# Shorter transposes for the inner attention tiles, and global probabilities sent behind the local ones, in a fused local/global attention and expert kernel

## The chip, the cores and the metric

The kernel runs on one core of one Trainium2 chip. The metric is the device time of one execution in microseconds (us). A comparison goes by the median of several executions; the kernel before was run three times. The profile comes from one further, recorded execution, whose own time is given beside its span below.

## The reference

There are 8 batches of 8 heads, 512 local tokens, 32 global tokens, head size 64, in float32. Global queries attend to all 544 keys, local queries to the 32 global keys and to the local keys within 32 positions. The rows of all heads are joined and sent through a layer with three first matrices (512 to 768), an elementwise maximum, and an output matrix (768 to 512).

```python
s_g = scale * np.matmul(q_g, k_all.transpose(0, 1, 3, 2))
out_g = np.matmul(sm(s_g), v_all)                     # sm: softmax over the last axis
s_ll = scale * np.matmul(q_l, k_l.transpose(0, 1, 3, 2))
s_ll = np.where(np.abs(pos[:, None] - pos[None, :]) <= 32, s_ll, -1000000000.0)
s_l = np.concatenate([scale * np.matmul(q_l, k_g.transpose(0, 1, 3, 2)), s_ll], axis=-1)
out_l = np.matmul(sm(s_l), np.concatenate([v_g, v_l], axis=2))
...
h = np.maximum(np.maximum(x @ w1, x @ w2), x @ w3)
return (h @ w_out).astype(np.float32)
```

## The kernel before

**Tiles.** Two heads form a pair; there are 32 pairs `p`, and each has 4 tiles `t` of 128 local queries, so 128 tiles `sl` in all, with `t = sl % 4` and `p = sl // 4` from tile 16 on. An outer tile (`t` = 0 or 3) sees 192 keys of each head, an inner tile (`t` = 1 or 2) 224. From pair 8 (tile 32) on, outer tiles are "mixed": the last 64 keys of both heads share one chunk of 128. An inner tile has two chunks for each head, one of 128 keys and one of 96; the other 32 columns of the second chunk meet rows of zeros in the packed values.

**Steps of a tile.** `scores` (L340) multiplies queries and keys on TensorE (L367), takes the masked minimum on VectorE (L370) and the exponential on ScalarE (L372), and scales by the reciprocal sum, mostly on GpSimd (`times`, L124). The result lies in `s`; from tile 16 on a DMA of SyncE's queue copies it into one of two `prob` buffers (L382 and L383 for mixed tiles, L385 for others), in the type that TensorE multiplies in one pass. `trans` (L389) transposes the four chunks of `prob` (three and one of global probabilities in some mixed tiles) into the PSUM bank `T` (L398, L401): the chunk is the loaded operand, the identity the streamed one. ScalarE or VectorE copies `T` to `pt` (L111, L109), VectorE stores the rounding rest beside it (L103). `pv` (L440) multiplies `pt` with the values on TensorE (L464).

**Global queries.** `glob` (L282) computes a pair's global scores in two steps into `sg`, of which there is one buffer; ScalarE copies the first part of each there (L111), VectorE finishes it (L302). `glob_soft` (L306) takes the exponential (L311) and GpSimd scales `sg` (L124). `glob_put` (L328) moves six pieces of `sg` (the table `GPUT`, L45) into the three chunks of a `probg` buffer with 7 DMAs of SyncE's queue (L335, and two at L338). `transg` (L413) transposes chunk 0, 1 or 2 of `probg` (L423) for the tile that comes next: chunk 0 for `t` = 0 and 2, chunk 1 for `t` = 1, chunk 2 for `t` = 3 (L401).

**Order.** The main loop (L585 on) is written tile by tile: in tile `sl` it transposes tile `sl + 1`, computes the scores of tile `sl + 3`, loads and splits operands, multiplies tile `sl` with its values, does a step of the next pair's global scores, and transposes the global probabilities of tile `sl + 1`. Between these steps `fill(n)` puts 4, 4, 3 and 7 matmuls of the expert layer of the batch before (`moe_group`, L503 for the first matrices and L522 for the output), so TensorE has independent work while the other engines make the operands. At the end of each batch of 16 tiles `fill(400)` empties the layer's remaining matmuls. A planner (`least`, L88) picks the engine of each copy, subtraction and scaling by summed costs as the program is written. Waits and the final order on each engine's queue come from the tile framework, which orders instructions by when its own model finds them ready; so two DMAs of SyncE may stand in another order than in the text. SyncE's queue starts its DMAs strictly one after the other, each waiting for its data.

In tile `t` = 2 the loop calls `glob_soft(p + 1)` and sends pieces 0 and 3; in tile `t` = 3 it sends pieces 1, 2, 4 and 5.

Of the kernel before, what the change touches and what calls it, by code (L numbers as in the profile page):

```python
# [10 lines left out]
F32 = mybir.dt.float32  # L11
# [10 lines left out]
NP = H // 2  # L22
# [28 lines left out]
def mixed(p, t):  # L51
    return p >= 2 * NP and t in (0, 3)


def f32(ap):
    return ap.bitcast(F32)


def body(ctx, tc, kin, qin, vin, min_, win, out):
    nc = tc.nc  # L60
    act, dve, pool, pe = nc.scalar, nc.vector, nc.gpsimd, nc.tensor
# [7 lines left out]
    psT = ctx.enter_context(tc.tile_pool(name="psT", bufs=1, space=PSUM))  # L69
# [15 lines left out]
    def spend(e, ns):  # L85
        load[e] += ns
# [18 lines left out]
    def copy(out, a, psum=False):  # L105
        n = width(out)
        c = {"d": n * (1.04 if psum else 0.52) + (160 if psum else 150), "a": n * 0.833 + (150 if psum else 190)}
        if least(c) == "d":
            dve.tensor_copy(out=out, in_=a)  # L109
        else:  # L110
            act.copy(out=out, in_=a)  # L111

    def times(out, a, col, move=False):
        n = width(out)
        c = {"d": n * 0.52 + 125, "a": n * 0.833 + 185}
        if not move:
            c["p"] = n * 1.27 + 150
        e = least(c)
        if e == "d":
            dve.tensor_scalar(out=out, in0=a, scalar1=col, scalar2=None, op0=ALU.mult)  # L120
        elif e == "a":
            act.activation(out=out, in_=a, func=AF.Copy, scale=col)
        else:
            pool.tensor_scalar(out=out, in0=a, scalar1=col, scalar2=1.0, op0=ALU.mult, op1=ALU.mult)  # L124
# [95 lines left out]
    def nat_k(p):  # L220
        if p < NP:
            return kn[p // 2][:, p % 2], qg[0][:, p]
        return kraw[p][:, 0:KW], kraw[p][:, KW:]
# [104 lines left out]
    def glob_put(p, which):  # L328
        if p >= B * NP:
            return  # L330
        s, g = pg[p][0], f32(pgt[p])
        for k in which:
            c0, n, i, h, d0 = GPUT[k]
            if k < 5 or p < 2 * NP:
                nc.sync.dma_start(out=g[64 * h:64 * h + 64, i, d0:d0 + n], in_=s[:, c0:c0 + n])  # L335
            else:
                for j in range(2):
                    nc.sync.dma_start(out=g[64:64 + SG, 2, 64 * j:64 * j + 64], in_=s[SG * j:SG * j + SG, 480:544])  # L338

    def scores(i):  # L340
        if i >= NS:
            return
        sl = ORDER[i]
        p, t = divmod(sl, 4)
        c0, n = WIN[t]

        ps = pm.tile([128, 512], F32, name="pm") if i < 8 else psS.tile([128, 512], F32, name="S")
        s = s4[:, i % 4]
        if i < EARLY:
            sc[i] = s  # L350
        else:
            if len(prob) < 2:
                prob.append(const.tile([128, 2, 256], F32R, name="prob", tag=f"prob{2 + len(prob)}"))
                pool.memset(f32(prob[-1]), 0.0)
            sc[i] = prob[i % 2]
        nm = small.tile([128, 2], F32, name="nm")
        z = small.tile([128, 2], F32, name="z")
        ze = z8[:, i % 4]
        ph = [ps[:, 0:224], ps[:, 224:448]]
        for j in range(2):  # L360
            if i in NATK:

                pe.matmul(ph[j][:, 0:n], lhsT=qraw[i][:, 128 * j:128 * j + 128], rhs=nat_k(p)[0][:, c0:c0 + n],  # L363
                          start=True, stop=True)
                continue
            for a in range(2):
                pe.matmul(ph[j][:, 0:n], lhsT=qs[i][:, a, 128 * j:128 * j + 128],  # L367
                          rhs=kst[p][:, j, c0:c0 + n], start=(a == 0), stop=(a == 1))
        for j in range(2):
            dve.tensor_tensor_reduce(out=s[:, j, 0:n], in0=ph[j][:, 0:n], in1=mask[:, (1, 0, 1, 0)[t], 32 * (t == 0):32 * (t == 0) + n],  # L370
                                     scale=-0.125, scalar=3.0e38, op0=ALU.add, op1=ALU.min, accum_out=nm[:, j:j + 1])
            act.activation(out=s[:, j, 0:n], in_=s[:, j, 0:n], func=AF.Exp, bias=nm[:, j:j + 1], scale=-1.0,  # L372
                           accum_out=ze[:, j, 0:1])
        dve.tensor_reduce(out=z, in_=ze, axis=AX.X, op=ALU.add)
        dve.reciprocal(out=z, in_=z)
        for j in range(2):
            times(s[:, j, 0:n], s[:, j, 0:n], z[:, j:j + 1])
        if i >= EARLY:
            d = f32(sc[i])
            if mixed(p, t):  # L380
                d = d.rearrange("p j x -> p (j x)")
                nc.sync.dma_start(out=d[:, 0:256].rearrange("p (j x) -> p j x", j=2), in_=s[:, :, 0:128])  # L382
                nc.sync.dma_start(out=d[:, 256:384].rearrange("p (j x) -> p j x", j=2), in_=s[:, :, 128:192])  # L383
            else:
                nc.sync.dma_start(out=d[:, :, 0:n], in_=s[:, :, 0:n])  # L385
        spend("d", 2 * (n * 1.04 + 220) + 440)
        spend("a", 2 * (n * 0.833 + 278))

    def trans(sl):  # L389
        if sl >= NS:  # L390
            return
        s = sc.pop(sl)
        ps = psT.tile([128, 512], F32, name="T")
        pr, one = (ps, ident) if sl < EARLY else (ps.bitcast(F32R), identr)
        m = 3 if mixed(*divmod(ORDER[sl], 4)) else 4
        s = s.rearrange("p j x -> p (j x)")
        for x in range(m):
            pe.transpose(pr[:, 128 * x:128 * x + 128], s[:, 128 * x:128 * x + 128], one)  # L398
        p, t = divmod(ORDER[sl], 4)
        if t == 3 and mixed(p, t):  # L400
            pe.transpose(pr[:, 384:512], pgt[p][:, 2], identr)  # L401
        src = ps.rearrange("p (x q) -> p x q", q=128)[:, 0:m]
        if sl < NAT:
            pt = pts[sl] = att.tile([128, 4, 160], F32, name="pt", tag="pt")
            copy(pt[:, 0:m, 0:128], src, True)
        else:
            pt = pts[sl] = att.tile([128, 4, 2, 160], F32R, name="pt", tag="pt")
            copy(pt[:, 0:m, 0, 0:128], src, True)
            sub(pt[:, 0:m, 1, 0:128], src, f32(pt)[:, 0:m, 0, 0:128], True)
        if t == 3 and mixed(p, t):  # L410
            transg(sl, ps[:, 384:512])
# [173 lines left out]
    for sl in range(NS):  # L585
        p, t = divmod(ORDER[sl], 4)
        b = p // NP
        settle(4500)
        if sl == 8:
            mm[0] = moe_local(0, 0, 256)  # L590
        elif sl == 16:
            mm[0] = chain(mm[0], moe_local(0, 256, 256))
        elif sl >= 32 and sl % 16 == 0:
            fill(400)
            mm[0] = moe_local(b - 1)
        n = (7, 6, 5, 9) if sl < 16 else (4, 4, 3, 7)
        trans(sl + 1)
        fill(n[0])
        next_scores(sl + 4 if sl < 12 else max(15, sl + 3))
        if sl >= 16:  # L600
            if t == 2:
                split_k(p + 2)
                load_k(p + 3)
        elif sl in (10, 14):
            load_k(sl // 4 + 2)
        elif sl == 15:
            load_k(6)
        fill(n[1])
        pv(sl)
        if sl < 8:  # L610
            if p < 3:
                if t == 0:
                    glob(p + 1, 0)
                    glob(p + 1, 1)
                else:
                    glob_soft(p + 1)
        elif sl < 16:
            if sl in (12, 13):
                glob(NP, sl - 12)
            elif sl == 14:  # L620
                glob_soft(NP)
        elif t <= 1:
            glob(p + 1, t)
        elif t == 2:
            glob_soft(p + 1)
            if p + 1 >= 2 * NP:
                glob_put(p + 1, (0, 3))
        elif p + 1 >= 2 * NP:
            glob_put(p + 1, (1, 2, 4, 5))
        fill(n[2])  # L630
        transg(sl + 1)
        fill(n[3])
        split_v(sl + 2)
        load_v(sl + 4)
        for _ in range(WS[sl] if sl < len(WS) else 0):
            weight_step()
        if sl < 8:
            if t == 1:
                xs.setdefault(0, []).append(split_x(xr[p][:, 0:2, 0:128]))
        elif sl < 16:  # L640
            if t == 3:
                split_x(xr[p][:, 2:4, 0:128], xs[0][p], 256)
        elif sl % 16 >= 12:
            q = b * NP + sl % 16 - 12
            xs.setdefault(b, []).append(split_x(xr[q][:, :, 0:128]))
# [60 lines left out]
```

## Time and profile before

| | |
|---|---|
| three runs | median 834.85 us (832.93 to 837.02) |
| the profiled execution, its own time | 834.52 us |
| its span, first to last instruction | 832.7 us |
| TensorE matmuls (PE) | 803.1 us busy, 96% of the span |
| TensorE operand loads (PEld) | 680.7 us, 82% |
| VectorE (DVE), ScalarE (ACT), GpSimd (POOL) | 61%, 63%, 62% |
| DMA, all engines | 114 GB/s in the mean |

Read it so: lines with PE are matmuls, with PEld the loading of the operand that stays in the array (they overlap matmuls), SPq is SyncE's queue of DMA issues. In a timeline each line has the start, the length in us, the engine, the line of the kernel, the operation, output and inputs, the shape and a count of merged instructions; a bracket at the end gives idle time before it and what ended it. Matmuls are pipelined, so a line's length is longer than its share of TensorE; the distance from one start to the next is what it costs. The expert layer runs beside attention until about 726 us; after that TensorE has only the layer of the last batch and of the global rows.

### The profile page before, as it was taken

Reading aid. Unit: us, or ns where it says so; the run is one execution under the profiler, and the core shown is the slowest. Engines: PE = TensorE matmul, PEld = TensorE weight load, DVE = VectorE, ACT = ScalarE, POOL = GpSimd, SP = SyncE. Lnnn points to the kernel's source line nnn. Section 1 sums busy time; section 2 is a strip of 40 time slices with the busy share of each in tenths; the row PEclk is TensorE's granted clock in tenths of the full one; section 3 lists DMA queues with packets and bytes.
Section 4 is the critical chain, followed back from the end, with each engine's and each line's share of the span. In section 5 each row is a group of like instructions: output and inputs, shape, how many; then the busy total and the mean of one; then the engine's idle time right before and its main releaser. Section 6 shows DMA issues by size and latency. Waiting matters only on the chain.

```text
span 832.7 us, 16036 instructions
## 1 busy us (share of the span) xinstructions
PE 803.1 (96%) x4620; PEld 680.7 (82%) x4620; DVE 511.4 (61%) x1789; ACT 522.3 (63%) x1495; POOL 513.2 (62%) x725
## 2 busy tenths in 40 slices
PE   7779899899999999999999999999999999999997
PEld 5469789878888888888888888878888888888896
DVE  3778744866776677766775766767666676411121
ACT  5788756777676767776676677776776666411111
POOL 4689836786677667867676676866776664311211
PEclk9999999999999999999999999999999999999999
DMA  7566544443344433343335333443335332100001
GB/s 251 174 221 221 186 148 122 132 133 110 110 115 129 117 104 112 100 149 104 103 106 165 111 96 102 125 127 99 105 93 165 115 86 57 59 13 0 26 26 26
DMA packets 106856, 94.58 MB, mean 114 GB/s; under 512 B 31888, under 2 KB 95248, under 8 KB 106768
## 3 DMA queue, kind: packets, MB, share of 16 engines
q1 hardware_dynamic: 106768, 93.56, 37.2%
q8 instruction: 37, 0.61, 0.3%
q14 instruction: 51, 0.42, 0.2%
HBM read 56.85 MB, written 8.91 MB: 79 GB/s over the span
## 4 chain that ended last, share of the span: by engine, by line
PE 81%; DVE 2%; DMA 1%; issue 1%; ACT 1%; POOL 1%; POOLq 0%; DVEq 0%; ACTq 0%
PE pm L503 48%; PE pm L522 15%; PE O L464 6%; PE S L367 5%; PE T L398 3%; PE S L298 2%; DMA prob<-s 1%; PE S L363 1%; PE O L457 1%; PE S L423 1%; ACT s L372 0%; DMA probg<-sg 0%; DVE s L370 0%; PE T L401 0%; DMA qraw<-q_in 0%
## 5 line engine op out<-in xcount | busy, mean ns | idle before, releaser
L503 PE MATMUL pm<-xs,wh 128*128 128x512 f32 (+1 forms) x1440 | 421.8, 368 | 5.5 <-ACT xs L111 2.4
L503 PEld LDWEIGHTS pm<-xs,wh 128*128 128x128 f32 x1440 | 253.3, 189 | 36.6 <-ACT xs L111 2.9
L503 PE MATMUL pm<-xs,wl 128*128 128x512 f32 (+1 forms) x720 | 264.1, 367 | 1.0 <-POOL wl L177 1.0
L503 PEld LDWEIGHTS pm<-xs,wl 128*128 128x128 f32 x720 | 136.3, 189 | 20.9 <-issue 1.6
L124 POOL TENSOR_SCALAR s<-s,z 128x224 f32<-128x224 f32 (+1 forms) x244 | 104.0, 438 | 67.7 <-ACT lox L111 38.7
L522 PE MATMUL pm<-woh,h 128*128 128x512 f32 x408 | 133.4, 398 | 0.9 <-POOL h L103 0.9
L372 ACT ACTIVATE s<-s,nm 128x224 f32<-128x224 f32 (+1 forms) x256 | 118.0, 462 | 19.2 <-DVE nm L370 18.0
L103 POOL TENSOR_TENSOR h<-m,h 128x512 fp32r<-128x512 f32 (+1 forms) x60 | 68.3, 1138 | 98.4 <-ACT h L111 98.2
L511 DVE TENSOR_TENSOR m<-pm,m 128x512 f32<-128x512 f32 (+1 forms) x120 | 72.9, 608 | 71.1 <-PE pm L503 70.7
L103 DVE TENSOR_TENSOR pt<-T,pt 128x512 fp32r<-128x512 f32 (+2 forms) x126 | 70.2, 557 | 72.1 <-ACT pt L111 71.7
L103 POOL TENSOR_TENSOR qs<-qraw,qs 128x256 fp32r<-128x256 f32 x100 | 73.0, 738 | 57.0 <-ACT qs L111 41.9
L370 DVE CUSTOM_DVE_ANT_0 s<-S,mask 128x224 f32<-128x224 f32 (+1 forms) x240 | 80.5, 369 | 28.3 <-PE S L363 17.0
L522 PEld LDWEIGHTS pm<-woh,h 128*128 128x128 f32 x408 | 74.5, 188 | 14.0 <-POOL h L103 1.7
L111 ACT CAST pt<-T 128x512 fp32r<-128x512 f32 (+2 forms) x117 | 55.6, 476 | 48.1 <-PE T L398 41.9
L522 PE MATMUL pm<-wol,h 128*128 128x512 f32 x204 | 81.8, 401 | 1.2 <-POOL wol L177 1.2
L103 POOL TENSOR_TENSOR kst<-kraw,kst 64x576 fp32r<-64x576 f32 x50 | 71.6, 1431 | 14.0 <-DVE nm L370 7.9
L103 POOL TENSOR_TENSOR vs<-vraw,vs 128x256 fp32r<-128x256 f32 x102 | 75.5, 740 | 6.4 <-ACT vs L111 4.8
L464 PEld LDWEIGHTS O<-pt,vs 128*128 128x128 f32 x408 | 66.0, 188 | 8.6
L464 PE MATMUL O<-pt,vs 128*128 128x320 f32 (+1 forms) x408 | 72.8, 300 | 0.0
L111 ACT CAST qs<-qraw 128x256 fp32r<-128x256 f32 x99 | 40.2, 407 | 48.4 <-PE S L367 45.9
L367 PEld LDWEIGHTS S<-kst,qs 128*128 128x128 f32 x400 | 59.6, 190 | 9.1 <-DVE nmg L302 0.6
L111 ACT CAST h<-m 128x512 fp32r<-128x512 f32 (+1 forms) x60 | 33.4, 556 | 53.3 <-DVE m L511 53.3
(99 smaller groups left out, 1228.2 us busy)
## 6 DMA issues: line engine op xcount, KB each, us to landing
vraw<-v_in SPq DMA_DIRECT2D x64, 256.0 KB, 3.2
qraw<-q_in SPq DMA_DIRECT2D x100, 128.0 KB, 2.2
prob<-s SPq DMA_DIRECT2D x56, 224.0 KB, 2.4
wraw<-w_in SPq DMA_DIRECT2D x24, 512.0 KB, 3.6
out_dram<-o SPq DMA_DIRECT2D x32, 256.0 KB, 2.6
kraw<-k_in SPq DMA_DIRECT2D x25, 320.0 KB, 3.4
prob<-s SPq DMA_DIRECT2D x48, 128.0 KB, 2.2
prob<-s SPq DMA_DIRECT2D x48, 64.0 KB, 2.0
```

The costliest lines, as they stand in the source:

```text
L103: (dve if least(c) == "d" else pool).tensor_tensor(out=out, in0=a, in1=b, op=ALU.subtract)
L111: act.copy(out=out, in_=a)
L124: pool.tensor_scalar(out=out, in0=a, scalar1=col, scalar2=1.0, op0=ALU.mult, op1=ALU.mult)
L298: pe.matmul(ps[:, 0:n], lhsT=qgz.rearrange("p j x -> p (j x)")[:, 128 * j:128 * j + 128], rhs=kst[p][:, j, c0:c0 + n], start=(j == 0), sto ...
L367: pe.matmul(ph[j][:, 0:n], lhsT=qs[i][:, a, 128 * j:128 * j + 128], rhs=kst[p][:, j, c0:c0 + n], start=(a == 0), stop=(a == 1))
L370: dve.tensor_tensor_reduce(out=s[:, j, 0:n], in0=ph[j][:, 0:n], in1=mask[:, (1, 0, 1, 0)[t], 32 * (t == 0):32 * (t == 0) + n], scale=-0.12 ...
L372: act.activation(out=s[:, j, 0:n], in_=s[:, j, 0:n], func=AF.Exp, bias=nm[:, j:j + 1], scale=-1.0, accum_out=ze[:, j, 0:1])
L398: pe.transpose(pr[:, 128 * x:128 * x + 128], s[:, 128 * x:128 * x + 128], one)
L464: pe.matmul(o[:, j, 0:320].rearrange("p (a q) -> p a q", a=2)[:, :, 0:n], lhsT=vs[sl][:, 2 * j + c].rearrange("p a d -> p (a d)"), rhs=pt[ ...
L503: pe.matmul(ps[:, 0:n], lhsT=w[f][:, i, k], rhs=xs[k][:, a, c0:c0 + n], start=(q == 0), stop=(q == 11))
L511: dve.tensor_tensor(out=m[:, 0:n], in0=ps[:, 0:n], in1=m[:, 0:n], op=ALU.max)
L522: pe.matmul(ps, lhsT=hh[f][:, a, 128 * t:128 * t + 128], rhs=w[:, f], start=(q == 0), stop=(q == 17))
```

## The change

From tile 34 on an inner tile's two second chunks (`x` odd, four chunks in all) are transposed with 96 loaded columns in place of 128, and the result fills 96 partitions of `T`. The copies out of `T` still read 128 partitions, so the bank must hold finite numbers there: from tile 32 on the same `T` tile is used again and again rather than a new one being allocated each time, and tile 33 still writes all rows.

The DMA of a tile's probabilities is remembered (`sent`). For pairs from 8 on, pieces 1 and 4 of the global probabilities become one DMA. Pieces 0 and 3 are sent in tile `t` = 2 as before. Pieces 1 with 4, and 2, now are sent in tile `t` = 2 too, but on SyncE's queue behind the DMA of the local probabilities of tile `sl + 3` (which is `t` = 1 of the next pair); piece 5 (two DMAs) is sent in tile `t` = 3, behind those of the tile after that. `tc.issue_after` orders the issue on that queue only; it waits for no data.

```diff
@@ glob_put
             c0, n, i, h, d0 = GPUT[k]
+            if k == 1 and p >= 2 * NP:
+                nc.sync.dma_start(out=g[0:64, 1:3, 32:128], in_=s[:, 0:512].rearrange("p (i x) -> p i x", i=2)[:, :, 128:224])
+                continue
             if k < 5 or p < 2 * NP:
...
+    sent = [None]
...
@@ scores
-                nc.sync.dma_start(out=d[:, 256:384].rearrange("p (j x) -> p j x", j=2), in_=s[:, :, 128:192])
+                sent[0] = nc.sync.dma_start(out=d[:, 256:384].rearrange("p (j x) -> p j x", j=2), in_=s[:, :, 128:192])
             else:
-                nc.sync.dma_start(out=d[:, :, 0:n], in_=s[:, :, 0:n])
+                sent[0] = nc.sync.dma_start(out=d[:, :, 0:n], in_=s[:, :, 0:n])
...
@@ trans
-        ps = psT.tile([128, 512], F32, name="T")
+        if sl <= 32:
+            bank[0] = psT.tile([128, 512], F32, name="T")
+        ps = bank[0]
...
-            pe.transpose(pr[:, 128 * x:128 * x + 128], s[:, 128 * x:128 * x + 128], one)
+            w = 96 if sl >= 34 and m == 4 and x % 2 else 128
+            pe.transpose(pr[0:w, 128 * x:128 * x + 128], s[:, 128 * x:128 * x + w], one)
...
@@ main loop
             if p + 1 >= 2 * NP:
                 glob_put(p + 1, (0, 3))
+                with tc.issue_after(sent[0].ins):
+                    glob_put(p + 1, (1, 2))
         elif p + 1 >= 2 * NP:
-            glob_put(p + 1, (1, 2, 4, 5))
+            with tc.issue_after(sent[0].ins):
+                glob_put(p + 1, (5,))
```

More of the change, by code (lines that the diff above doesn't have):

```diff
@@ L382, in scores @@
                 nc.sync.dma_start(out=d[:, 0:256].rearrange("p (j x) -> p j x", j=2), in_=s[:, :, 0:128])
-                nc.sync.dma_start(out=d[:, 256:384].rearrange("p (j x) -> p j x", j=2), in_=s[:, :, 128:192])
+                sent[0] = nc.sync.dma_start(out=d[:, 256:384].rearrange("p (j x) -> p j x", j=2), in_=s[:, :, 128:192])
             else:
-                nc.sync.dma_start(out=d[:, :, 0:n], in_=s[:, :, 0:n])
+                sent[0] = nc.sync.dma_start(out=d[:, :, 0:n], in_=s[:, :, 0:n])
         spend("d", 2 * (n * 1.04 + 220) + 440)
         spend("a", 2 * (n * 0.833 + 278))
+    bank = [None]
     def trans(sl):
```

## The prediction

> **What bounds the kernel now.** I read the page first: busy shares, granted clock, the chain.
>
> ```profile
> span 832.7 us, 16036 instructions
> PE 803.1 (96%) x4620; PEld 680.7 (82%) x4620; DVE 511.4 (61%) x1789; ACT 522.3 (63%) x1495; POOL 513.2 (62%) x725
> PEclk9999999999999999999999999999999999999999
> PE 81%; DVE 2%; DMA 1%; issue 1%; ACT 1%; POOL 1%; POOLq 0%; DVEq 0%; ACTq 0%
> ```
>
> TensorE holds 96% of the span and 81% of the chain at full clock; the others are near 62%. The change touches the stretch from tile 32 on, so I asked the windows view for 200 to 700 us, ten stretches of 50.
>
> ```profile
> sum 500.00, PE 498.12 PEld 422.36 DVE 347.21 ACT 351.45 POOL 345.69; mean PE 49.81 PEld 42.24 DVE 34.72 ACT 35.15 POOL 34.57
> ```
>
> Of 500 us TensorE stands still for 1.88. So no wait that ends earlier can give much, and a gain must come from these stalls or from TensorE's own instructions. The TensorE timeline shows the stalls: three of 0.3 us or more, all ahead of the transposes of an inner tile with t = 1 at the end of a batch. I lay an undisturbed tile beside them, and the tiles' single transposes.
>
> ```profile
> 411.45 0.22 PE L423 MATMUL S<-identr,probg 128*128 128x128 f32 x1
> 411.51 0.45 PE L503 MATMUL pm<-xs,wl 128*128 128x512 f32 x1
> 411.80 0.63 PE L503 MATMUL pm<-xs,wh 128*128 128x512 f32 x2
> 412.26 0.39 PE L503 MATMUL pm<-xs,wl 128*128 128x512 f32 x1
> ...
> 412.95 0.40 PE L503 MATMUL pm<-xs,wl 128*128 128x512 f32 x1
> 413.19 0.46 PE L398 MATMUL T<-identr,prob 128*128 128x128 f32 x4
> 413.49 0.70 PE L503 MATMUL pm<-xs,wh 128*128 128x512 f32 x2
> 414.02 0.39 PE L503 MATMUL pm<-xs,wl 128*128 128x512 f32 x1
> ...
> 452.79 0.39 PE L522 MATMUL pm<-wol,h 128*128 128x512 f32 x1
> 453.71 0.51 PE L398 MATMUL T<-identr,prob 128*128 128x128 f32 x4 [0.54 <-DMA prob<-s]
> ...
> 545.17 0.39 PE L522 MATMUL pm<-wol,h 128*128 128x512 f32 x1
> 546.69 0.51 PE L398 MATMUL T<-identr,prob 128*128 128x128 f32 x4 [1.14 <-DMA prob<-s]
> ...
> 638.41 0.40 PE L522 MATMUL pm<-wol,h 128*128 128x512 f32 x1
> 639.00 0.51 PE L398 MATMUL T<-identr,prob 128*128 128x128 f32 x4 [0.20 <-DVE xs L109]
> ```
>
> An expert matmul ahead of transposes takes 413.19 - 412.95 = 0.24 us. The three stalls are the excess over that: 0.92 - 0.24 = 0.68, 1.52 - 0.24 = 1.28 and 0.59 - 0.24 = 0.35, together 2.31 us. These are tiles 81, 97 and 113.
>
> **The global transfers.** SyncE's queue and the scaling on GpSimd around tile 81, the issues of tiles 97 and 113, and how long the transfers take from issue to landing (minimum, median, maximum; local ones first):
>
> ```profile
> 445.35 3.78 SPq L335 DMA_DIRECT2D probg<-sg  x5
> 449.17 1.23 SPq L338 DMA_DIRECT2D probg<-sg  x2
> 450.50 0.53 SPq L260 DMA_DIRECT2D qraw<-q_in  x1
> 451.13 0.68 SPq L385 DMA_DIRECT2D prob<-s  x1
> ...
> 446.64 0.88 POOL L124 TENSOR_SCALAR s<-s,z 128x224 f32<-128x224 f32 x2
> ...
> 543.85 0.68 SPq L385 DMA_DIRECT2D prob<-s  x1
> ...
> 636.41 0.68 SPq L385 DMA_DIRECT2D prob<-s  x1
> ...
> DMA to landing us min/median/max: 2.0/2.3/5.3
> ...
> DMA to landing us min/median/max: 1.7/1.9/4.7
> ```
>
> GpSimd has tile 81's probabilities ready at 446.64 + 0.88 = 447.52, but the queue sends them at 451.13, behind seven global transfers and a load: 3.61 us late. The transposes start 453.71 - 451.13 = 2.58 after the issue, tile 113's 639.00 - 636.41 = 2.59 and tile 97's 2.84: the same distance, so tile 113 waits for its transfer too, though the row puts it down to another engine. The change leaves pieces 0 and 3 ahead and puts the rest behind, so tile 81 is sent at 447.52 and lands near 447.52 + 2.45 = 450.0, where TensorE could take it at 452.79 + 0.24 = 453.03: 3 us in hand. I take all three stalls away, -2.31 us (end of the bound: nothing, if another wait takes their place, below). What is late next is TensorE itself, since the expert matmuls are in its queue.
>
> What moves, and what it passes. Of seven issues per pair two stay, one merged DMA and piece 2 go behind the t = 1 transfer, and piece 5's two behind the t = 2 transfer, on SyncE's queue alone; GpSimd's scaling of sg is not moved. The merged DMA saves one issue, 0.6 us of SyncE by the rows above (1.23 for two); no user is left that waits for the queue's pace, so it counts nothing. Pieces 1, 2 and 4 are issued by about 448.2 + 2 x 0.6 = 449.4 and land by 451.3; their first user, the t = 1 tile's global transpose, comes 411.45 - 407.22 = 4.23 us after its transposes by the next rows, so near 457.3: 6 us in hand. Piece 5 is the one that becomes late, with who waits for it:
>
> ```profile
> 406.42 0.65 SPq L385 DMA_DIRECT2D prob<-s  x1
> 407.19 0.54 SPq L272 DMA_DIRECT2D vraw<-v_in  x1
> ...
> 407.22 0.45 PE L398 MATMUL T<-identr,prob 128*128 128x128 f32 x4
> ...
> 411.35 0.47 ACT L111 COPY sg<-S 64x384 f32<-64x384 f32 x1
> 413.69 0.59 ACT L111 CAST pt<-T 128x512 fp32r<-128x512 f32 x1
> ...
> 414.31 0.69 DVE L103 TENSOR_TENSOR pt<-T,pt 128x512 fp32r<-128x512 f32 x1 [1.18 <-ACT pt L111]
> ...
> 415.85 0.74 PE L464 MATMUL O<-pt,vs 128*128 128x320 f32 x4
> ```
>
> The one sg buffer is written again by ScalarE at 411.35, and that copy now has to wait until piece 5 has been read. Piece 5's second issue starts at 406.42 + 0.65 + 0.61 = 407.68, or 408.22 behind the load of vraw, and lands 1.9 later, at 409.6 to 410.1: 1.2 us ahead of the copy. Queued behind the copy on ScalarE is the cast of 413.69; VectorE's subtraction ends at 415.00 and TensorE needs it at 415.85, another 0.85. So zero, with 2 us of cover.
>
> **The 96 columns.** Affected are 47 inner tiles (tile 34, and two in each of the 23 pairs 9 to 31), 2 transposes each, 94. The loaded chunk gets narrower; the streamed identity keeps 128 columns, so only the load can gain. What a transpose costs: one alone 0.06 to the next matmul, and that one then 0.29 in place of 0.46 / 2 = 0.23, so 0.12 us. Four: 0.30, and the pair behind takes 414.02 - 413.49 = 0.53 in place of 0.46, so 0.37. Each further transpose costs (0.37 - 0.12) / 3 = 83 ns, more than the 60 ns that the streaming of a single one takes: the loads pace them. Load times by width, from the groups by shape:
>
> ```profile
> L503 PEld LDWEIGHTS pm<-xs,wh 128*128 128x128 f32 x1440 | 253.3, 189 | 36.6 <-ACT xs L111 2.9 <-POOL xs L103 2.6 <-issue 2.1
> L398 PEld LDWEIGHTS T<-identr,prob 128*128 128x128 f32 x400 | 45.9, 141 | 21.0 <-DVE xs L109 2.5 <-issue 1.8 <-DVE xr L472 1.4
> L457 PEld LDWEIGHTS O<-pt,vraw 128*64 128x64 f32 x208 | 12.7, 139 | 6.2 <-ACT pt L111 2.4 <-issue 1.4 <-ACT wct L162 0.2
> L398 PEld LDWEIGHTS T<-ident,s 128*128 128x128 f32 x64 | 7.3, 142 | 2.7 <-issue 2.5 <-ACT pt L111 0.2
> ```
>
> Loads of ordinary matmuls: 189 for 128 columns, 139 for 64, so 0.78 ns a column on a fixed 89. A transpose's 141 is then 89 + 52, or 0.41 a column. No row has a transpose of 96. Upper end of the gain: the ordinary price, 32 x 0.78 = 25 ns, 94 of them 2.35 us. Lower end: the narrower load falls back to the ordinary load's pace, 89 + 96 x 0.78 = 164, which is 23 ns more, +2.2 us. I take the transpose's own price, since the row is this very instruction: 32 x 0.41 = 13 ns, -1.2 us. The Trainium skill (TensorE: Matmul & The Clock Gate, section LDWEIGHTS) prices a load at its columns over 1.2, by which 32 columns are 26.7 ns and the 94 are 2.5 us, an estimate, so that the sum would be -4.8; the 64-column row agrees with it for ordinary loads (0.78 a column), the transposes' 141 does not.
>
> The kept bank: a new T tile waits for the copies of the last, and the kept one waits for the same two readers. VectorE's subtraction of one tile ends at 415.00, and tiles come 413.19 - 407.22 = 5.97 us apart, so some 4 us hide it: zero. Copies, multiplications with the values and the expert layer keep their sizes.
>
> Sum against the profiled execution: 834.52 - 2.31 - 1.2 = 831.0. The median of the runs is 0.33 above that execution, so I forecast **831.4**, 0.42% less than 834.85. I call anything within 0.5% (4.2 us) no change, about what a measurement can tell here.
>
> **The rivals.**
> Faster (0.25): the load is priced by column as for ordinary matmuls. -2.31 - 2.35 = -4.66, 830.2. For it speaks that loads pace the transposes at 83 ns, a quarter of which is 21; against it the 141.
>
> Stalls change their name (0.11): at a batch's end another wait takes the place. For it: the bracket of 639.00 names the cast of xs. Against it: TensorE's first matmuls there read the first of four pieces of x. Only the 1.2 stays: 833.7.
>
> Narrow loads lose (0.11): the lower end, -2.31 + 2.2 = -0.1, 834.7. The Trainium skill (same page, section on weight-path perf modes) says that fast weight load is on only for 128 weights of a type other than FP32, by which 96 would lose it. The trace speaks against that cause: float32 transposes load in 142, the other type's in 141, and the 128-column load of L503 takes 189.
>
> Slower (0.08): piece 5 is too late for ScalarE. It decides once piece 5 lands after 411.35 + 0.85 = 412.2. With vraw ahead and the longest landing of the row, 408.22 + 4.7 = 412.9, so TensorE would wait 0.7 us in each of 23 pairs, 16.1 us: 834.85 + 16.1 - 3.5 = 847.5. For it: sg has one buffer, and the order on the queue is the framework's. Against it: a landing takes 1.9 in the median.
>
> **How the numbers follow.** The forecast has 0.45. Its 3.5 us lie 0.7 from the bound, and three runs of before spread from 832.93 to 837.02, so a median can be off by about 1: I count 0.1 of the forecast's share as faster. Faster 0.25 + 0.1 = 0.35; same 0.35 + 0.11 + 0.11 = 0.57; slower 0.08. The range reaches from the first rival less that 1 to the third plus 1: 829.2 to 835.7. It leaves out the slower rival and some of the ends.
>
> **What would show it.** Right: in the changed profile the three batch ends show 0.24 us ahead of the transposes, waits of L398 on prob are gone, SyncE sends L385 of t = 1 right when GpSimd ends, TensorE's idle time from 200 to 700 us falls below 0.5, and 96-column loads take near 128 ns. Wrong: loads of 164 or more; a wait of ScalarE's sg copy on a DMA and of L464 on pt; or stalls at 453, 545 and 638 us with another name. More than 5 us either way would mean that a cost which I set to zero is not.

## The result and the profile after

The kernel after took 828.88 us in the median of 6 runs (828.43 to 831.59), the kernel before 834.24 beside it (6 runs, 832.93 to 837.02). The ratio is 0.994, with a 95% interval from 0.9921 to 0.9958: 5.4 us less, or 0.6%, where 3.5 us were forecast. The profiled execution took 828.43 us. Its page begins:

```profile
span 826.6 us, 15915 instructions
...
PE 797.9 (97%) x4620; PEld 677.2 (82%) x4620; DVE 514.0 (62%) x1789; ACT 521.8 (63%) x1495; POOL 513.8 (62%) x725
...
PE 83%; DMA 1%; DVE 1%; ACT 1%; POOL 1%; issue 1%; POOLq 0%; ACTq 0%; DVEq 0%
```

TensorE still holds nearly all of the span with the same 4620 matmuls, and 83% of the chain; VectorE, ScalarE and GpSimd stay near 62%. What changed has to be read stage by stage. The windows view from 200 to 700 us, in stretches of 50, ends with:

```profile
sum 500.00, PE 499.93 PEld 424.20 DVE 350.65 ACT 353.68 POOL 346.79; mean PE 49.99 PEld 42.42 DVE 35.06 ACT 35.37 POOL 34.68
```

TensorE stands still for 0.07 us of 500, where it stood for 1.88 before. The three batch ends in TensorE's timeline:

```profile
449.83 0.39 PE L532 MATMUL pm<-wol,h 128*128 128x512 f32 x1
450.06 0.44 PE L408 MATMUL T<-identr,prob 128*128 128x128 f32 x4
...
541.47 0.39 PE L532 MATMUL pm<-wol,h 128*128 128x512 f32 x1
541.70 0.44 PE L408 MATMUL T<-identr,prob 128*128 128x128 f32 x4
...
633.11 0.39 PE L532 MATMUL pm<-wol,h 128*128 128x512 f32 x1
633.34 0.42 PE L408 MATMUL T<-identr,prob 128*128 128x128 f32 x4
```

(All line numbers behind L340 have moved by 5 to 10: the transposes' L398 is now L408.) Each transpose starts 0.23 us behind the expert matmul; before, it was 0.92, 1.52 and 0.59. SyncE's queue around the first of them, and GpSimd's scaling of that tile:

```profile
442.43 1.16 SPq L338 DMA_DIRECT2D probg<-sg  x2
443.68 0.55 SPq L260 DMA_DIRECT2D qraw<-q_in  x1
444.47 0.63 SPq L390 DMA_DIRECT2D prob<-s  x1
445.19 0.62 SPq L335 DMA_DIRECT2D probg<-sg  x1
445.86 1.23 SPq L338 DMA_DIRECT2D probg<-sg  x1
```

```profile
443.56 0.88 POOL L124 TENSOR_SCALAR s<-s,z 128x224 f32<-128x224 f32 x2
```

GpSimd ends at 443.56 + 0.88 = 444.44 and the transfer is sent at 444.47, 0.03 us later in place of 3.61. The merged piece (L335) and piece 2 stand behind it. The loads by shape, from 200 to 720 us (busy us, mean ns of one):

```profile
L408 PEld LDWEIGHTS T<-identr,prob 128*128 128x128 f32 x225 | 29.4, 141 | 8.5 <-DMA prob<-s 0.6
...
L408 PEld LDWEIGHTS T<-identr,prob 128*96 128x96 f32 x90 | 11.4, 126 | 4.0
```

A 96-column load takes 126 ns, a 128-column one still 141. The first row also shows something new, a wait for `prob`. It belongs to the batch's last tile (`t` = 3), whose probabilities come in two transfers; TensorE around it, and the queue:

```profile
438.59 0.39 PE L532 MATMUL pm<-wol,h 128*128 128x512 f32 x1
438.82 0.58 PE L408 MATMUL T<-identr,prob 128*128 128x128 f32 x3
439.24 0.25 PE L411 MATMUL T<-identr,probg 128*128 128x128 f32 x1
```

```profile
436.27 0.66 SPq L387 DMA_DIRECT2D prob<-s  x1
437.03 0.65 SPq L388 DMA_DIRECT2D prob<-s  x1
```

The first chunks are there in time. The third chunk comes with L388, issued at 437.03 right behind L387; it lands at 439.08, its load starts at 439.12, and TensorE waits in the middle of the tile: 439.24 - 438.82 = 0.42 us for three transposes, which elsewhere take 0.22. Four batch ends have it, and their excess of about 0.2 each sums to 0.8 us.

**Where the time went.** I cut the trace by the first multiplication with the values of tile 32 and of tile 127, which is nearly all that the change touches. Before, then after:

```profile
180.86 0.30 PE L464 MATMUL O<-pt,vs 128*128 128x320 f32 x1
...
725.37 0.30 PE L464 MATMUL O<-pt,vs 128*128 128x320 f32 x1
```

```profile
178.55 0.30 PE L474 MATMUL O<-pt,vs 128*128 128x320 f32 x1
...
719.53 0.30 PE L474 MATMUL O<-pt,vs 128*128 128x320 f32 x1
```

The stretch takes 544.51 before and 540.98 after, 3.53 us less. Another 2.31 lie ahead of tile 32, where the compute engines run the same instructions in both kernels; only SyncE's queue differs there, from 173 us on, by the transfers of pair 8. So in the stretch these two executions give what was forecast, and the 2.31 need an explanation of their own: chance, or something that the change does early on. The runs below settle that too.

### The profile page after: what moved, and what is told of

Read it like the earlier page. It is cut to its first block, busy times and chain, and to the rows that moved or that the text cites. A ratio compares the mean times of both kernels' runs of the same rounds, so it can differ in the third digit from the quotient of the medians.

```text
span 826.6 us, 15915 instructions
## 1 busy us (share of the span) xinstructions
PE 797.9 (97%) x4620; PEld 677.2 (82%) x4620; DVE 514.0 (62%) x1789; ACT 521.8 (63%) x1495; POOL 513.8 (62%) x725
## 4 chain that ended last, share of the span: by engine, by line
PE 83%; DMA 1%; DVE 1%; ACT 1%; POOL 1%; issue 1%; POOLq 0%; ACTq 0%; DVEq 0%
PE pm L513 48%; PE pm L532 16%; PE O L474 6%; PE S L372 5%; PE T L408 3%; PE S L298 1%; DMA prob<-s 1%; PE S L368 1%; PE S L433 1%; PE O L467 0%; ACT s L377 0%; PE T L411 0%; POOL s L124 0%; DVE kst L109 0%; PE S L294 0%
## 5 line engine op out<-in xcount | busy, mean ns | idle before, releaser
L474 PEld LDWEIGHTS O<-pt,vs 128*128 128x128 f32 x408 | 66.0, 188 | 8.5
L474 PE MATMUL O<-pt,vs 128*128 128x320 f32 (+1 forms) x408 | 72.7, 299 | 0.0
```

The costliest lines, as they stand in the source:

```text
L474: pe.matmul(o[:, j, 0:320].rearrange("p (a q) -> p a q", a=2)[:, :, 0:n], lhsT=vs[sl][:, 2 * j + c].rearrange("p a d -> p (a d)"), rhs=pt[ ...
```

## The experiments

**The change again, and its parts.** Four kernels were timed beside the kernel before (29 runs, median 834.75): the change as it is; the sending order alone; the narrow transposes with the kept bank alone; the kept bank alone.

> The whole change once more, beside the kernel before. Theory A (the sum of the prediction holds, -3.5 us, and what was measured beyond it lies ahead of tile 32, where no instruction differs, as spread between executions): from the first multiplication with values of tile 32 to that of tile 127 the trace is 3.3 to 3.8 us shorter than that of before (544.5 us), and the medians differ by 3 to 4.5 us. Rival B (the change is worth 5 to 6 us by itself): the medians differ by 5 us or more again, whatever the time of tile 32.

The order alone has the change's `glob_put` and main loop (the merged transfer is part of it and has no run of its own), with

```diff
-        if sl <= 32:
-            bank[0] = psT.tile([128, 512], F32, name="T")
-        ps = bank[0]
+        ps = psT.tile([128, 512], F32, name="T")
...
-            w = 96 if sl >= 34 and m == 4 and x % 2 else 128
+            w = 128
```

> The global transfers merged and sent behind the local ones; transposes with 128 columns and a new T bank for each tile, as before. Theory A: the three waits at the batch ends are gone, -2.3 us from tile 32 to tile 127, medians -2 to -3. Rival B1 (the extra gain comes from the transfers): -4 us or more. Rival C (the narrow transposes carry the gain, the stalls come back elsewhere): within 0.8 us of before.

The narrow transposes alone undo the sending:

```diff
-            if k == 1 and p >= 2 * NP:
-                nc.sync.dma_start(out=g[0:64, 1:3, 32:128], ...)
-                continue
...
-                with tc.issue_after(sent[0].ins):
-                    glob_put(p + 1, (1, 2))
...
-            with tc.issue_after(sent[0].ins):
-                glob_put(p + 1, (5,))
+            glob_put(p + 1, (1, 2, 4, 5))
```

> 96 columns and the kept bank; transfers in the order of before. Theory A: -1.2 us from tile 32 to 127 (13 ns for each of 94 loads), with the waits at the batch ends still there, longer by what TensorE is earlier. Rival B2 (narrow loads gain as much as ordinary ones, 25 ns or more): -2.4 us or more.

The kept bank alone is that kernel with `w = 128`.

> The T bank kept from tile 32 on, with 128 columns in all transposes and the transfers of before. Theory A: no change, within 0.5 us from tile 32 to 127. Rival B3 (a new bank for each tile costs a wait that the trace puts elsewhere): -1 us or more.

| kernel | median us (runs) | ratio to before, 95% | stretch, tile 32 to 127 | TensorE idle, 200 to 700 us |
|---|---|---|---|---|
| whole change | 829.05 (6) | 0.9932 [0.9908, 0.9955] | 541.42 | 0.07 |
| order alone | 831.74 (12) | 0.9961 [0.9945, 0.9977] | 542.03 | 0.00 |
| narrow, kept bank | 831.69 (12) | 0.9970 [0.9955, 0.9985] | 543.04 | 1.86 |
| kept bank alone | 833.26 (12) | 0.9987 [0.9970, 1.0004] | 544.66 | 2.06 |

The whole change is 5.7 us faster in the median, more than the 3 to 4.5 of theory A, while its stretch is only 544.51 - 541.42 = 3.09 shorter, less than the 3.3 of that theory. Both parts are worth something, and each leaves the other's cost standing: the order alone has no idle time at all, the narrow transposes alone keep batch ends' stalls (1.7 and 0.5 us in this trace). Here is the stall in the narrow kernel (TensorE's waits for 200 to 720 us: engine, line, releaser, us in total, times, longest):

```profile
PE T L405 <- DMA prob<-s: 1.5, 1, 1.5
```

The kept bank's 544.66 is the 544.51 of before again, and its interval reaches 1.0004, so no effect is established, although its median is 1.5 us lower.

**How much two executions of one kernel differ.** The kernel before was recorded three times more and the change twice more, to compare four traces with four.

> The kernel before, recorded a second time, to see how far one execution differs from another. Theory A (the changed stretch is steady, the start is not): tile 32 to tile 127 takes 544.5 us within 0.4 again, while tile 32 comes anywhere from 178.5 to 181 us. Rival B4 (the kernel before has a slower start than the others by itself): tile 0 again near 18.3 us and tile 32 near 180.9, where the five other traces have tile 0 at 15.9 to 16.6.

> The kernel before, a third recorded execution. Open is why the medians differ by 5.4 and 5.7 us where the recorded stretches from tile 32 to 127 differ by 3.1 to 4.3. Theory A: that stretch takes 544.5 to 545.3 us again, and an execution's total varies with when tile 32 comes (178.5 to 181). Rival B5 (some executions of the kernel before have longer waits ahead of the transposes, which the change removes): the stretch takes 546 us or more.

> The whole change, a third recorded execution. Theory A: 540.9 to 541.5 us from tile 32 to 127, tile 32 anywhere from 178.5 to 181. Rival B6 (the change also shortens the stretch ahead of tile 32): tile 32 below 179 us, as in the first recorded execution, and not near 180 as in the second.

> The kernel before, a fourth recorded execution, with the same two expectations as the third: Theory A 544.5 to 545.3 us from tile 32 to 127; rival B5 546 us or more.

> The whole change, a fourth recorded execution, with the same two expectations as the third: Theory A 540.9 to 541.5 us from tile 32 to 127 with tile 32 anywhere from 178.5 to 181; rival B6 tile 32 below 179 us.

| trace | start of tile 32 | stretch | batch-end stalls in it |
|---|---|---|---|
| before, recorded first | 180.86 | 544.51 | 2.36 |
| before, second | 179.41 | 545.24 | 3.06 |
| before, third | 181.06 | 544.96 | 2.86 |
| before, fourth | 178.97 | 546.19 | 4.12 |
| change, recorded first | 178.55 | 540.98 | 0 |
| change again | 180.06 | 541.42 | 0 |
| change, third | 178.62 | 541.28 | 0 |
| change, fourth | 180.82 | 541.28 | 0 |

Four things follow. Most of the start belongs to neither kernel: the kernel before has it at 178.97 and the change at 180.82. It goes with the early part of an execution, though no run shows that part as its cause. TensorE's granted clock from 20 to 100 us was 0.98 in the three traces with the earliest start (178.55, 178.62, 178.97) and 0.89 to 0.96 in the other five; and the first trace of before already began its first multiplication with values, that of tile 0, at 18.26 us, the seven others between 15.97 and 16.73. So of the first pair's 2.31 us, 1.93 were there at tile 0. (In the second trace of before tile 0 comes at 16.12, so the late start is not that kernel's own.)

A small part of the start is the change's. From the first multiplication with the values in `vs` (tile 26) to tile 32 the four traces of before, the narrow kernel and the kept bank take 32.11 to 32.18 us, the four of the change and the order alone 31.88 to 31.91. One more batch end lies there, ahead of the transposes of tile 33, before and then after:

```profile
177.74 0.40 PE L522 MATMUL pm<-wol,h 128*128 128x512 f32 x1
178.14 0.51 PE L398 MATMUL T<-identr,prob 128*128 128x128 f32 x4
```

```profile
175.65 0.39 PE L532 MATMUL pm<-wol,h 128*128 128x512 f32 x1
175.88 0.46 PE L408 MATMUL T<-identr,prob 128*128 128x128 f32 x4
```

The transfer of this tile is issued 2.50 us ahead of its transposes before (at 175.64) and 3.23 us ahead after (at 172.65). So 0.24 us of the gain lie ahead of tile 32. The stretch does belong to the kernels: 545.22 in the mean against 541.24, which is 3.98 us less, with the nearest two 3.09 apart. And the stalls of before are longer in every other trace than in the one on which the prediction was made: 3.10 in the mean of four. They are all that its traces differ by there: less its stalls each stretch takes 542.07 to 542.18 us. The fourth trace has a fourth stall, and 1.5 us at each of two others. These are TensorE's waits there, 200 to 720 us:

```profile
PE T L398 <- DMA prob<-s: 3.5, 4, 1.4
```

The whole spans differ by 4.7 us in the mean of four (832.55 and 827.88), which lies inside what the timed runs give, 3.5 to 6.6 us by the interval of the ratio; 0.6 of it lies in the start (0.24 by the change, the rest by chance), 0.1 behind tile 127. The traces thus give the change 4.3 us; the medians' 5.4 and 5.7 are about 1.2 more, which no trace locates.

**Piece 5 still later.** Its cover was set to 2 us without a trace of it. Six small transfers into a tile of zeros, each about 0.6 us of SyncE's queue, were put ahead of it:

```diff
+            for k in range(6):
+                with tc.issue_after(sent[0].ins):
+                    sent[0] = nc.sync.dma_start(out=zero[16 * k:16 * k + 16], in_=ident[16 * k:16 * k + 16, 127:128])
             with tc.issue_after(sent[0].ins):
                 glob_put(p + 1, (5,))
```

> The whole change, with six tiny transfers of 64 bytes put ahead of piece 5 on SyncE's queue, so that piece 5 is read some 3 to 3.6 us later. It tests the cover that the prediction gave that step: 1.2 us until ScalarE's copy into sg and 0.85 more until TensorE. Theory A: ScalarE's copy waits, TensorE stands 1.0 to 1.5 us in each of 23 pairs, 23 to 35 us more than the change. Rival D (ScalarE's work behind that copy has more room than the prediction saw): less than 5 us more.

It took 839.91 us in one run (before: 834.28), and its stretch 550.41, 9.2 more than the change's mean: 0.40 us in each of 23 pairs. Piece 5 without the delay, SyncE and then ScalarE in the change:

```profile
403.43 0.61 SPq L390 DMA_DIRECT2D prob<-s  x1
404.09 1.25 SPq L341 DMA_DIRECT2D probg<-sg  x2
```

```profile
408.33 0.48 ACT L111 COPY sg<-S 64x384 f32<-64x384 f32 x1
```

Its second issue starts at 404.09 + 0.62 = 404.71, 3.6 us ahead of the copy, and no wait stands before the copy. With the delay, SyncE, ScalarE, VectorE and TensorE:

```profile
390.96 1.22 SPq L643 DMA_DIRECT2D zero<-ident  x2
392.23 1.22 SPq L341 DMA_DIRECT2D probg<-sg  x2
```

```profile
394.89 0.48 ACT L111 COPY sg<-S 64x384 f32<-64x384 f32 x1 [1.76 <-DMA probg<-sg]
```

```profile
395.40 0.55 DVE L302 CUSTOM_DVE_ANT_0 sg<-S,sg 64x384 f32<-64x384 f32 x1 [2.08 <-ACT sg L111]
```

```profile
395.19 0.40 PE L513 MATMUL pm<-xs,wh 128*128 128x512 f32 x1
396.01 0.69 PE L372 MATMUL S<-kst,qs 128*128 128x192 f32 x4 [0.43 <-DVE nmg L302]
```

ScalarE stands 1.76 us for the transfer, VectorE for ScalarE, and TensorE 0.43 for VectorE, which frees the PSUM buffer `S` that the next tile's scores need. TensorE's multiplication with `pt` (L474), where the prediction saw the end of the cover, waits nowhere. The waits of all its loads ahead of those scores:

```profile
PEld S L372 <- DVE nmg L302: 12.0, 17, 1.0
```

So the chain is real and begins at the copy, but it reaches TensorE over another buffer. Of 3.7 us of delay 0.40 arrive, neither the full delay nor nothing: the 23 to 35 us of theory A were missed, and so were the less than 5 of rival D.

**All four chunks narrow.** `w = 96 if sl >= 34 and m == 4 else 128`: twice as many narrow loads. It leaves out the last 32 keys of each first chunk.

> The whole change, with 96 loaded columns in all four transposes of an inner tile in place of two. It leaves out the last 32 keys of each first chunk (their rows hold values of an earlier tile). Theory A (loads pace the transposes, 33 ns less per inner tile for two narrow loads): four narrow loads give up to as much again, 0.7 to 1.6 us less from tile 32 to 127. Rival E (the 60 ns of streaming is now the floor): within 0.3 us of the change.

It took 827.66 us in one run, its stretch 539.80, 1.4 less than the change's mean; the change's four traces spread over 0.44. The transposes and the two expert matmuls behind them, in the change and then here:

```profile
404.23 0.43 PE L408 MATMUL T<-identr,prob 128*128 128x128 f32 x4
404.50 0.69 PE L513 MATMUL pm<-xs,wh 128*128 128x512 f32 x2
405.03 0.40 PE L513 MATMUL pm<-xs,wl 128*128 128x512 f32 x1
```

```profile
410.35 0.41 PE L408 MATMUL T<-identr,prob 128*96 128x128 f32 x4
410.61 0.69 PE L513 MATMUL pm<-xs,wh 128*128 128x512 f32 x2
411.14 0.39 PE L513 MATMUL pm<-xs,wl 128*128 128x512 f32 x1
```

From the first transpose to the last row it was 414.02 - 413.19 = 0.83 us before; it is 0.80 with two narrow chunks and 0.79 with four. Over all inner tiles from 200 to 700 us the medians, start to start, up to the second matmul behind, are:

| loads | transposes and the first matmul behind, ns | up to the second matmul |
|---|---|---|
| four of 128 (before) | 60, 66, 84, 85, 302 | 600 |
| two of 96 (change) | 59, 60, 73, 70, 302 | 566 |
| four of 96 | 60, 62, 60, 64, 303 | 548 |

The first two narrow loads save 34 ns a tile, the next two only 18: with all four narrow every transpose follows in 60 to 64 ns, as long as the stream of one takes, and by these medians little is left to win from narrower loads. They account for 18 ns x 47 tiles = 0.85 of the 1.4 us; the rest is not located.

**The same two steps earlier.** Pairs 5 to 7 also send their later pieces behind the local transfer, the narrow chunks begin at tile 17, and the bank is kept from tile 16 on:

```diff
-        if p < 2 * NP:
+        if p == NP:
...
+        elif p < 2 * NP:
+            glob_put(p, (0, 3))
+            with tc.issue_after(sent[0].ins):
+                glob_put(p, (1, 2, 4, 5))
...
-            w = 96 if sl >= 34 and m == 4 and x % 2 else 128
+            w = 96 if sl >= 17 and ORDER[sl] % 4 in (1, 2) and x % 2 else 128
```

> The whole change, and the same two steps for earlier tiles: narrow transposes from tile 17 on, and for pairs 5 to 7 pieces 1, 2, 4 and 5 issued behind the local transfer. In the trace of the change tile 29's probabilities wait 1.45 us behind two global transfers, and TensorE stands 0.9 us for them. Theory A: that stall goes, and 16 narrow loads give 0.25 us: 0.5 to 1.2 us less than the change. Rival F (ahead of tile 32 other engines set the pace): no difference to the change within 0.4 us.

829.90 us (6 runs), a ratio to before of 0.9943 [0.9925, 0.9961]: no better than the change. Tile 32 starts at 181.00 us, in the span of the other starts, and the stretch behind it takes 540.75. TensorE's waits from 140 to 178 us, in the change and then here:

```profile
PE T L408 <- DMA prob<-s: 2.5, 4, 1.0
PE pm L532 <- POOL h L103: 0.9, 1, 0.9
PE S L372 <- DVE nmg L302: 0.4, 1, 0.4
```

```profile
PE T L412 <- DMA prob<-s: 1.9, 2, 1.1
PE T L412 <- ACT pt L111: 1.7, 1, 1.7
PE pm L536 <- POOL h L103: 1.0, 1, 1.0
```

Two of the four waits on the transfer go, and one of 1.7 us on ScalarE's copy takes their place. From tile 26 to tile 32 this trace takes 30.76 us, 1.1 less than the change's four, but the 1.7 us wait stands ahead of tile 26, and from 143.3 to 146.8 us TensorE's granted clock was 0.51. So a local gain is there, and it does not reach the median of six runs; in this early part other engines are late too.

## Why the prediction was right in its mechanism and short in its sum

**The three stalls: right, and too small.** The transfer goes out right behind GpSimd, the stalls are gone in all four traces of the change, and the order alone removes them. The -2.31 us were those of one trace; the mean of four is -3.10. The fourth batch end, at 178 us, lies ahead of the 200 us from which the prediction looked, and adds 0.24. The row at 639.00, which the prediction read as a wait for the transfer although its bracket names an engine, went with the others. The rival in which a stall only changes its name has no row in its favour at those tiles; at `t` = 3 it has 0.6 us, as follows.

**What is late next: missed.** The prediction said that TensorE itself is next, since the first user had 3 us in hand. It looked at the tiles with `t` = 1 alone, and it put SyncE's pace under the new order at nothing. The batch's last tile now gets its second transfer too late, four times 0.2 us. Two things add up there. With the new order the two transfers of a `t` = 3 tile are issued more slowly; these are the ones of the same tile before:

```profile
439.37 0.59 SPq L382 DMA_DIRECT2D prob<-s  x1
440.05 0.59 SPq L383 DMA_DIRECT2D prob<-s  x1
```

The second follows the first by 0.69 us there, by 437.03 - 436.27 = 0.76 in the change, and its landing moves back by 0.12 against the end of GpSimd's scaling. Why the issues became longer (0.59 to 0.66), no run shows. And with narrow loads TensorE arrives 0.03 to 0.08 us earlier. Means over the four batch ends, in us:

| kernel | landing behind GpSimd's end | transposes start behind it | excess of the `t` = 3 transposes over their median time, summed |
|---|---|---|---|
| before, four traces | 2.70 | 2.60 to 2.62 | 0.13 to 0.22 |
| kept bank alone | 2.70 | 2.59 | 0.26 |
| narrow, kept bank | 2.70 | 2.55 | 0.39 |
| order alone | 2.82 | 2.61 | 0.63 |
| change, four traces | 2.82 to 2.83 | 2.56 to 2.57 | 0.79 to 0.82 |
| all four narrow | 2.82 | 2.53 | 0.94 |

In the order alone TensorE starts no earlier than before, so there the whole excess comes from the later landing.

**The narrow loads: right, and near in size.** 126 ns were measured, 128 foretold. But the prediction took only the load's own difference, 13 ns, and 94 of them; in the chain of starts each is worth 17, for the transposes behind each other are paced by the loads: 34 ns x 47 tiles = 1.6 us in place of 1.2. That is the upper end of what the runs say. The narrow kernel's stretch is 544.66 - 543.04 = 1.6 below the kept bank's, but 0.4 of it are shorter stalls in its trace and 0.1 go into longer waits at `t` = 3, which leaves 1.3 to 1.4; the change against the order alone gives 542.03 - 541.24 + 0.2 = 1.0. So 1.2 lies inside. The ordinary price of 25 ns a load was not reached. It was drawn from two rows of different types, too: the 64-column load has float32 operands (`vraw`), the 128-column one does not. By the Trainium skill (TensorE: Matmul & The Clock Gate, section LDWEIGHTS) 32 columns fewer save 26.7 ns, an estimate; the rows give 141 - 126 = 15, so the trace does not agree for transposes. The rival after the Trainium skill (same page, section on weight-path perf modes), that fewer than 128 weights load more slowly, has fallen with the same 126.

**Two zeros held.** The kept bank is not told apart from nothing. Piece 5 costs nothing as it is sent now. Its cover is there, but it ends at another place than the prediction named: at the scores that wait for `S`, not at L474; and when it is used up, TensorE loses a part of the delay rather than all of it.

**The sum.** -3.1 for the stalls, -1.0 to -1.6 for the loads, +0.6 for the new waits (0.8 less the 0.2 that before has in the mean) make -3.5 to -4.1; the stretch gives 541.24 - 545.22 = -3.98, and 0.24 come ahead of it. The forecast had -3.5. What failed is the size of the first term, and the missing third one offset most of it. That the first two traces gave 3.53 was luck: against the same trace of the change the other three of before give 3.98 to 5.21. The median of 828.88 lies 0.3 under the range; 834.85 times the ratio, 829.8, lies inside it. The likeliest outcome of the forecast, no change, was narrowly missed: 0.6%, with an interval from 0.4 to 0.8% that holds the bound of 0.5. The order alone came out 0.5 us better in its one trace than its terms make (3.19 against 3.10 less 0.45 of new waits). Less their stalls the traces of before agree within 0.11 us, so this is not their spread; it stays open, and with it whether the loads are worth 1.0 or 1.6.

## What to carry to other kernels

Where a queue issues strictly in order, look for transfers that have 6 us in hand standing ahead of one that the bounding engine waits for, and price the fix by the stalls of several recorded executions: a stall's place mostly repeats, its length doesn't. When such a stall goes, follow the next tiles' transfers too: the new order can make one of them land later, and the engine may arrive earlier at it. Narrower loads pay where start-to-start times show that loads pace the engine, and only down to the time of the stream.

## What was not expected of the hardware

- A group of transposes costs more than its starts show: whatever the loads' width, the first 512-column expert matmul behind it takes 302 ns to the next one, where 231 are usual. Narrow loads did not change this.
- A 96-column load is 15 ns shorter, but shortens the chain by 17.
- Code that differs by 0.24 us up to tile 32 ended between 178.55 and 181.06 us in the eight traces of the two kernels, the earliest three with the highest granted clock from 20 to 100 us. A difference of 2 us between two single traces can therefore be nothing; cutting the trace at the change's first tile removes it.
- The two transfers of a `t` = 3 tile took 0.64 to 0.67 us each of SyncE's queue in the kernels with the new order, 0.59 to 0.61 in the others (both issued right behind each other, 200 to 720 us), and at the batch ends the second landed 0.12 us later behind its data.
